# Four weight columns of a dense layer by seven products instead of eight, in four of six token groups

## The chip, the cores and the metric

The kernel runs on one core of one Trainium2 chip. The metric is the device time of one execution in microseconds. One execution was taken by the hardware profiler; its events are what the profile shows. The engines are named as in the profile: PE (TensorE, matrix multiplication), PEld (its weight loads, which overlap with PE), DVE (VectorE), ACT (ScalarE), POOL (GpSimd) and SP (SyncE, here only a queue of DMAs). Each engine takes its own instructions in the order in which the program lists them.

## The reference

A linear attention with decay (4 batches, 8 heads, 768 tokens, head size 64) and, on its output, a two-layer network with the Mish activation.

```
for each block of 64 tokens:
    intra = (q k^T * Dmask) v                  # Dmask = lam^(i-j) for i >= j
    inter = (q * lam^(pos+1)) kv_state
    out   = intra + inter
    kv_state = lam^64 * kv_state + (k * lam^(63-pos))^T v
x = out, heads joined                           # 3072 tokens x 512
h = x @ w_in                                    # 512 x 2048, the first dense layer
g = h * tanh(softplus(h))                       # Mish
result = g @ w_out                              # 2048 x 512, the second dense layer
```

## The kernel before

The tokens are cut into six groups (n = 0 to 5) of 128 positions x 4 batches = 512 tokens. The kernel's attention works on blocks of 128 positions, so a group is four chunks (i = 4n + b), one for each batch. `xt[n]` holds the attention's output of group n, turned so that the 512 model columns lie on partitions (4 chunks of 128, `kc`). `hsg[n]` holds the first layer's output after Mish: 16 units of 128 columns, times 512 tokens.

**Order.** The program is written out by hand (`tc.manual_schedule()`): the order in which the Python code calls things is the order on each engine. The main loop over groups goes through a list `units`, and after unit u it does the other work that is due there.

**A group, n of 1 to 5, before.** Units 0 to 7 are *duos* (`mm1_duo`): two of the 16 column units (2g and 2g+1) for the first half of the tokens, 8 matmuls of 256 columns into one PSUM bank, then one Mish on ACT. Units 8 to 15 are the same for the second half of the tokens. Units 16 to 29 are the second layer (`fast_unit`): it is done already by seven products P1 to P7 instead of eight (Strassen's scheme in Winograd's form, over halves of the tokens, the inner dimension and the columns), in the order P1, P5, P6, P2, P7, P3, P4, each as two blocks of 8 matmuls. It needs sums of weights (`tsum`, `weight_sum`, once) and of activations (`gsum`, `token_sum`, each group), which DVE makes. Partial results are copied by ACT from one PSUM bank to another, on which the next product then accumulates, for example `z<-x` after P1 and `y<-z` after P6.

**Attention for the next group** lies between the units (`visit`, `turns`). `turn(i)` scales one chunk of k on DVE (`scale_k`) and issues two transposing DMAs on SP (`qraw`, `kraw`). `pair_s` does the scores of two chunks: 16 matmuls into four PSUM banks, 16 more into `pO` from the state, and four masks (`sb`) on DVE. `pair_o` adds the values: 16 matmuls, four DVE operations (`xtok`) and two transposing DMAs into `xt`. `pair_a` brings the state forward: 8 matmuls into two banks (`pv`), four DVE sums of them with the old state (`raw`) and one more (`state`).

**PSUM** is eight banks, given out by tags: "ph" (2), "po" (2), "pS", "pk", "pO", "pq" (1 each). A tag's next tile waits until the one before is read. In units below 15, `pair_s` and `pair_a` use the two "po" banks (`spare`); `pair_s` uses "pS" and "pk" for its first chunk.

**Group 0** has whole units of 512 tokens (`mm1_unit`) and is preceded by the first attention chunks (`look_t`, `look_s`, `look_o`, `look_kv`), in which PE often waits for ACT and DVE; short matmuls on zeros (`busy`) fill such waits. The weight sums `tsum` are made by DVE around units 14 to 23 of group 0. Inputs and weights are loaded by POOL's DMA queue; `pace()` lets POOL wait for a marker in `hsg` before later loads.

Of the kernel before, what the change touches and what calls it, by code (L numbers as in the profile page):

```python
# [7 lines left out]
F32 = mybir.dt.float32  # L8
# [12 lines left out]
def kernel(  # L21
# [12 lines left out]
    C = 128  # L34
# [166 lines left out]
    kq = {}  # L201
    sbs = {}

    def look_t(i, between=0, mid=None):

        out_ = []
        for src, name in ((k0 if i == 0 else kn[i] if i < B else ktil[i], "pk"),
                          (q0 if i == 0 else qn[i], "pq")):
            pt = ps.tile([128, JP, C], F16, name=name, tag=name)
            for j in range(JP):  # L210
                nc.tensor.matmul(
                    pt[:, j, :], src[:, 2 * j : 2 * j + 2, :].rearrange("p h c -> p (h c)"), ident,
                    is_transpose=True, start=(j == 0), stop=(j == JP - 1),
                )
            out_.append(work.tile([128, JP, C], F16, name=f"{name}T", tag=f"{name}T", bufs=2))
            if name == "pk" and between:
                busy(between, C)
            if name == "pq" and mid:
                mid()
            if name == "pq" and i >= B:  # L220
                nc.vector.tensor_tensor(out=out_[-1], in0=pt, in1=lq, op=ALU.mult)
            elif name == "pq" and i in (0, 3):
                nc.vector.tensor_copy(out_[-1], pt)
            else:
                nc.scalar.activation(out_[-1], pt, AF.Copy)
        kq[i] = out_

    def look_s(i, hold=False):

        kT, qT = kq[i]  # L230
        pS = [ps.tile([128, JP, C], F32, name="pS", tag=g, bufs=m)
              for g, m in (("pS", 1), ("po", 2) if i < B else ("pk", 1))]
        for j in range(JP):
            for t in range(2):
                rs = slice(64 * t, 64 * t + 64)
                nc.tensor.matmul(pS[t][:, j, :], kT[rs, j, :], qT[rs, j, :],  # L236
                                 start=(j == 0), stop=(j == JP - 1), skip_group_check=True)
        sbs[i] = [None, None]

        def mask(t):  # L240
            sbs[i][t] = work.tile([128, JP, C], F16, name="sb", tag="sb", bufs=4)
            nc.vector.tensor_tensor(out=sbs[i][t], in0=pS[t],
                                    in1=dm[:, t] if i < B else bc(maskT, 1, JP), op=ALU.mult)

        masks = [lambda t=t: mask(t) for t in ((0, 1) if i < B else (1, 0))]
        if hold:
            return masks
        for f in masks:
            f()

    def look_o(i):

# [208 lines left out]
    def weight_sum(i, s):  # L461
# [7 lines left out]
        )[i]  # L469
        nc.vector.tensor_tensor(out=tsum[i][:, ks, :], in0=a, in1=b, op=op)  # L470

    gsum = {}

    def token_sum(n, i, part):

        if (n, i) not in gsum:
            gsum[n, i] = work.tile([128, HK, 2 * C], F16, name=f"gsum{i}", tag=f"gsum{i}", bufs=1)
        w = HK // 2
        ks = slice(part * w, part * w + w)
        kh = slice(HK + part * w, HK + part * w + w)  # L480
        h = hsg[n]
        lo, hi = slice(0, 2 * C), slice(2 * C, 4 * C)
        a, b, op = (
            lambda: (h[:, ks, hi], h[:, kh, hi], ALU.add),
            lambda: (gsum[n, 0][:, ks, :], h[:, ks, lo], ALU.subtract),
            lambda: (h[:, ks, lo], h[:, ks, hi], ALU.subtract),
            lambda: (h[:, kh, lo], gsum[n, 1][:, ks, :], ALU.subtract),
        )[i]()
        nc.vector.tensor_tensor(out=gsum[n, i][:, ks, :], in0=a, in1=b, op=op)  # L489
# [118 lines left out]
    busy(3)  # L608
    look_s(1)
    q_powers()  # L610
    for hp in range(2):
        rs = slice(64 * hp, 64 * hp + 64)
        nc.vector.tensor_copy(lbm[rs, :, rs], bc(lbc[rs, :], 2, D))
    look_o(0)
    look_t(2)
    q_decays()
    busy(2)
    masks = look_s(2, hold=True)
    look_o(1)
    look_t(3, mid=masks[0])  # L620
    masks[1]()
    nc.scalar.preload_act_table(AF.Mish)
    busy(1)
    look_s(3)
# [3 lines left out]
    look_o(3)  # L628
    for i in range(1, B):
        scale_k(i)  # L630
    summed()
    busy(2)

# [8 lines left out]
    for u, (fn, args) in enumerate(units):  # L642
        put_off = []
        fn(*args, **({"then": put_off} if u in (23, 25) else {}))
        if u < B - 1:
            look_kv(u + 1, "pq" if u == 0 else "po")()
        if 8 <= u < 8 + NVB - B:
            nc.vector.memset(vz[u - 8 + B][:, :, D : 2 * D], 0.0)
        elif u == 13:
            nc.vector.tensor_scalar(out=maskT, in0=rel, scalar1=0.0, scalar2=None, op0=ALU.is_ge)  # L650
        for i, s in {14: ((0, 0),), 15: ((0, 1),), 18: ((1, 0), (2, 0)),
                     20: ((1, 1), (2, 1))}.get(u, ()):
            weight_sum(i, s)
        for i, part in sums.get(u, ()):
            token_sum(0, i, part)
        if u == 22:
            scale_k(4)
            weight_sum(3, 0)
        then = [f(i, "po" if i == 5 else "ph") if f is look_kv else f(i) for f, i in visit.get(u, ())]
        if u == 23:  # L660
            scale_k(5)
            scale_k(6)
            weight_sum(3, 1)
        for f in put_off + then:
            if f:
                f()
        if u in (25, 26, 27):
            for _ in range(2):
                ahead.pop(0)()
        if u == 26:  # L670
            scale_k(7)
    next_state(1, 0)

    for n in range(1, NG):
        r, s, t = Pair(), Pair(), Pair()
        r.n, r.bs, s.n, s.bs, t.n, t.bs = n, (2, 3), n + 1, (0, 1), n + 1, (2, 3)
        visit = {}
        if n > 1:
            visit[0] = pair_o, last
        if 1 < n < NG - 1:  # L680
            visit[5] = pair_a, r
        if n < NG - 1:
            visit[9 if n > 1 else 11] = pair_s, s
            visit[16] = pair_o, s
            visit[26] = pair_s, t
        if n < NG - 2:
            visit[21] = pair_a, s
        last = t
        turns = {23: (n + 2) * B, 25: (n + 2) * B + 1}
        turns.update({1: 9, 4: 10, 7: 11} if n == 1 else {3: (n + 1) * B + 2, 6: (n + 1) * B + 3})  # L690
        units = [(mm1_duo, (n, g, lo, lo + GT // 2)) for lo in (0, GT // 2) for g in range(NKI // 2)]
        steps = ("P1", "P5", "P6", "P2", "P7", "P3", "P4")
        units += [(fast_unit, (n, step, blk)) for step in steps for blk in range(2)]
# [5 lines left out]
        sums = {9: ((2, 0),), 11: ((2, 1),), NKI - 3: ((0, 0), (1, 0)), NKI - 1: ((0, 1), (1, 1)),  # L699
                NKI + 4: ((3, 0),), NKI + 5: ((3, 1),)}  # L700
        for u, (fn, args) in enumerate(units):
            fn(*args)
# [11 lines left out]
            if later and (8 <= u < 16 or u in (17, 19, 21, 23)):  # L714
                pace()
                later.pop(0)()
            for i, part in sums.get(u, ()):
                token_sum(n, i, part)
            if turns.get(u, NG * B) < NG * B:
                turn(turns[u])  # L720
            if u in visit:
                f, s_ = visit[u]
                s_.spare = ("po", "po") if u < NKI - 1 else ("pS", "pk") if f is pair_a else ("ph", "po")
                f(s_)


# [28 lines left out]
```

## Time and profile before

| | |
|---|---|
| median of 3 runs (lowest, highest) | 201.9 us (201.06, 202.19) |
| profiled execution | 201.82 us |
| its span, from the first to the last instruction | 200.0 us |
| outside the span | 1.82 us |
| granted PE clock over the span | 1.00 |
| busy: PE, PEld, DVE, ACT, POOL | 192.7, 161.0, 132.7, 91.7, 81.7 us |

On the chain of waits, group 1 begins at 50.5 us, group 2 at 81.0, group 3 at 110.8, group 4 at 140.7 and group 5 at 170.0; the last matmul ends at 196.8. A row of the groups of instructions reads: line, engine, operation, out<-in with shapes, count | busy us, mean ns of one | idle time of the engine just before them, and what ended it. A row of the timeline or of the chain begins with its start and its length in us. "x4" in a timeline row means four instructions merged, whose length runs from the first start to the last end.

### The profile page before, as it was taken

Reading aid. Unit: us, or ns where it says so; the run is one execution under the profiler, and the core shown is the slowest. Engines: PE = TensorE matmul, PEld = TensorE weight load, DVE = VectorE, ACT = ScalarE, POOL = GpSimd, SP = SyncE. Lnnn points to the kernel's source line nnn. Section 1 sums busy time; section 2 is a strip of 40 time slices with the busy share of each in tenths; the row PEclk is TensorE's granted clock in tenths of the full one; section 3 lists DMA queues with packets and bytes.
Section 4 is the critical chain, followed back from the end, with each engine's and each line's share of the span. In section 5 each row is a group of like instructions: output and inputs, shape, how many; then the busy total and the mean of one; then the engine's idle time right before and its main releaser. Section 6 shows DMA issues by size and latency. Waiting matters only on the chain.

```text
span 200.0 us, 5052 instructions
## 1 busy us (share of the span) xinstructions
PE 192.7 (96%) x2081; PEld 161.0 (80%) x2081; DVE 132.7 (66%) x251; ACT 91.7 (46%) x158; POOL 81.7 (41%) x129
## 2 busy tenths in 40 slices
PE   7969999999999999999999999999999999999993
PEld 3645447878888998998998998998998988988882
DVE  7798359799935978657878557878557827305513
ACT  5694674323665421465420565430565430666230
POOL 7996333778488862007982007982000000000000
PEclk9999999999999999999999999999999999999999
DMA  9999999999999999999999959999991023500014
GB/s 131 143 143 194 206 207 202 154 173 198 194 102 151 158 149 165 176 241 71 109 140 198 231 106 79 99 103 178 267 120 35 0 56 105 156 6 0 3 52 157
DMA packets 112457, 26.81 MB, mean 134 GB/s; under 512 B 101554, under 2 KB 112434, under 8 KB 112434
## 3 DMA queue, kind: packets, MB, share of 16 engines
q0 software_dynamic: 77552, 13.37, 98.7%
q1 hardware_dynamic: 30848, 9.97, 29.4%
q10 hardware_dynamic: 4034, 3.15, 5.5%
q8 instruction: 16, 0.26, 0.6%
q14 instruction: 7, 0.06, 0.1%
HBM read 27.26 MB, written 6.29 MB: 168 GB/s over the span
## 4 chain that ended last, share of the span: by engine, by line
PE 93%; DVE 3%; ACT 2%; issue 0%; ACTq 0%
PE ph L443 35%; PE z L503 14%; PE x L503 10%; PE ph L414 7%; PE y L503 6%; PE w L503 5%; PE pS L358 2%; PE pO L264 2%; PE pO L385 2%; PE pS L236 1%; PE pv L337 1%; DVE dm L177 1%; PE busy L157 1%; PE pO L366 1%; PE pv L311 1%; PE fin L578 1%
## 5 line engine op out<-in xcount | busy, mean ns | idle before, releaser
L443 PE MATMUL ph<-xt,win 128*128 128x256 f16 x640 | 72.9, 273 | 0.0
L443 PEld LDWEIGHTS <-win 128*128 128x128 f16 x640 | 61.6, 98 | 7.4
L450 ACT ACTIVATE hsg<-ph 128x512 f16<-128x512 f32 x80 | 47.8, 597 | 29.3 <-PE ph L443 29.2
L503 PEld LDWEIGHTS <-gsum 128*128 128x128 f16 x384 | 36.9, 98 | 4.8 <-DVE tsum L470 0.3
L489 DVE TENSOR_TENSOR gsum<-hsg 128x1024 f16<-128x1024 f16 x24 | 16.6, 691 | 23.8 <-ACT hsg L450 18.5
L503 PEld LDWEIGHTS <-hsg 128*128 128x128 f16 x272 | 26.1, 98 | 3.2
L503 PE MATMUL x<-wout,hsg 128*128 128x256 f16 x192 | 23.7, 273 | 0.0
L67 POOL DMA_DIRECT2D kn<-in_k_dram x23 | 20.6, 894 | 7.4 <-DMA win<-in_moe_w_in_dram 2.2
L503 PE MATMUL z<-tsum,gsum 128*128 128x256 f16 x192 | 23.3, 273 | 0.0
L405 POOL COPY paced<-hsg 1x1 f16<-1x1 f16 x33 | 10.4, 314 | 31.5 <-ACT hsg L450 31.5
L75 POOL DMA_DIRECT2D qn<-in_q_dram x23 | 20.4, 888 | 6.0 <-DMA wout<-in_moe_w_out_dram 3.3
L78 POOL DMA_DIRECT2D vz<-in_v_dram x24 | 21.2, 886 | 3.4 <-DMA wout<-in_moe_w_out_dram 1.7
L374 DVE TENSOR_TENSOR sb<-pS,maskT 128x512 f16<-128x512 f32 x32 | 19.9, 684 | 1.0 <-PE pS L358 0.7
L297 DVE TENSOR_TENSOR raw<-pv,state 64x256 f32<-64x256 f32 x24 | 10.1, 422 | 12.8 <-PE pv L337 12.5
L274 DVE TENSOR_TENSOR ktil<-kn,lk 128x512 f16<-128x512 f16 (+1 forms) x22 | 14.9, 684 | 3.0 <-DMA kn<-in_k_dram 3.0
L414 PE MATMUL ph<-xt,win 128*128 128x512 f16 x64 | 14.5, 379 | 0.3 <-ACT xt L266 0.3
L393 DVE TENSOR_TENSOR xtok<-pO,lqt 128x256 f16<-128x256 f32 x32 | 11.3, 416 | 3.9 <-PE pO L385 3.9
L560 ACT ACTIVATE osum<-z 128x512 f32<-128x512 f32 x5 | 3.0, 597 | 23.6 <-PE z L503 23.6
L530 DVE TENSOR_TENSOR osum<-z,p 128x512 f32<-128x512 f32 x6 | 4.1, 690 | 12.9 <-issue 6.8
L503 PE MATMUL y<-wout,gsum 128*128 128x256 f16 x96 | 12.3, 273 | 0.0
L426 ACT ACTIVATE hsg<-ph 128x512 f16<-128x512 f32 x16 | 9.6, 597 | 5.8 <-PE ph L414 5.8
L414 PEld LDWEIGHTS <-win 128*128 128x128 f16 x64 | 6.1, 98 | 7.3 <-issue 0.4
(93 smaller groups left out, 209.0 us busy)
## 6 DMA issues: line engine op xcount, KB each, us to landing
vz<-in_v_dram POOLq DMA_DIRECT2D x24, 128.0 KB, 6.8
out_dram<-osum SPq DMA_DIRECT2D x12, 256.0 KB, 5.2
kn<-in_k_dram POOLq DMA_DIRECT2D x23, 128.0 KB, 5.8
qn<-in_q_dram POOLq DMA_DIRECT2D x23, 128.0 KB, 5.8
out_dram<-osum ACTq DMA_DIRECT2D x11, 256.0 KB, 4.6
wout<-in_moe_w_out_dram POOLq DMA_DIRECT2D x4, 512.0 KB, 16.7
win<-in_moe_w_in_dram POOLq DMA_DIRECT2D x3, 512.0 KB, 10.3
win<-in_moe_w_in_dram POOLq DMA_DIRECT2D x2, 256.0 KB, 6.4
```

Of the source, the lines that this page charges most:

```text
L67: nc.gpsimd.dma_start(out=kn[i], in_=chunk_rows(k, i))
L75: nc.gpsimd.dma_start(out=qn[i], in_=chunk_rows(q, i))
L78: nc.gpsimd.dma_start(out=vz[i % NVB][:, :, 0:D], in_=chunk_rows(v, i))
L274: (nc.gpsimd if B + 1 < i < 2 * B else nc.vector).tensor_tensor(out=t, in0=kn[i], in1=bc(lk, 2, D), op=ALU.mult)
L374: nc.vector.tensor_tensor(out=s.sb[m][t], in0=sc[m][t], in1=bc(maskT, 1, JP), op=ALU.mult)
L393: nc.vector.tensor_tensor(out=xtok[m][:, :, t, :], in0=s.pO[t][:, m], in1=bc(lt[:, :, t], 2, D), op=ALU.mult)
L405: nc.gpsimd.tensor_copy(paced, mark[-1])
L414: nc.tensor.matmul(ph_t[ni][:, lo:hi], w_in(ni, kc), xt[n][:, kc, lo:hi], start=(kc == 0), stop=(kc == NKC - 1),)
L443: nc.tensor.matmul(t[:, m, lo - half * h : hi - half * h], w_in(ni, kc), xt[n][:, kc, lo:hi], start=(m == 0 and kc == 0), stop=(kc == NKC ...
L450: nc.scalar.activation(hsg[n][:, 2 * g : 2 * g + 2, half * h : half * h + h], t, AF.Mish)
L489: nc.vector.tensor_tensor(out=gsum[n, i][:, ks, :], in0=a, in1=b, op=op)
L503: nc.tensor.matmul(places(n, key)[:, blk, lo:hi], lhs(kk, blk), rhs(kk, lo, hi), start=(fresh and kk == 0 and blk == 0), stop=(kk == HK - ...
```

## The change

In groups 2 to 5, column units 12 to 15 (the weight tile `win1536`, 512 x 512) are no longer four duos of the list. They are one 512 x 512 x 512 multiplication by seven products, `set_unit`, in the same scheme as the second layer: halves of the tokens, of the inner dimension and of the columns. A product is 4 matmuls of 256 columns. Group 1 keeps its duos.

- `in_sum` makes four weight sums (128 x 512 elements, f16) on DVE once, in group 0 after unit 12, ahead of `tsum`.
- `x_sum` makes four sums of `xt` (128 x 512, f16) on DVE in each of the groups, two after unit 6 and two after unit 8, behind that unit's visit.
- The group has 28 list entries: 0 to 3 duos of the first half; 4 is P1 and a duo, 5 is P2 and a duo; 6 to 9 duos of the second half; 10 is P5 and P6, 11 a duo, 12 is P7 and P3, 13 a duo and P4; 14 to 27 the second layer.
- Copies on ACT: after P1 the bank x to SBUF (`u1`); after P5 the bank w to SBUF (`p5`); ahead of P6 `u1` into bank z; after P6 bank z into bank y. Then P7 and P4 accumulate on z, P3 on y. DVE adds `p5` to z after P7 and to y after P3 (`hs`), and Mish reads those sums; after P2 and P4 it reads the bank itself.
- Visits move to fit: `pair_s` for the next group's first pair comes after unit 6 (it was 9), with `pair_a` after unit 5 as before. The closing `pair_o` of the second pair comes after the last unit of a group, and no longer after unit 0 of the next. The second `turn` comes after unit 5 (it was 6), and the token sums of the halves come together after unit 13.
- In the opening, the two `lbm` copies on DVE move from before `look_o(0)` to behind the first `scale_k`, and both masks of chunk 2 stand together ahead of the pq copy of chunk 3 (one stood behind it). `weight_sum(3, 1)` moves from unit 23 to unit 25 of group 0.

The diff, cut to its core:

```diff
-    def look_t(i, between=0, mid=None):
+    def look_t(i, between=0):
...
-            if name == "pq" and mid:
-                mid()
...
+    KH = NKC // 2
+    SU = NKI - 4
+    isum = [const.tile([128, KH, 256], F16, name=f"isum{i}") for i in range(4)]
+    def i_quarter(r, c):
+        t = win[-1]
+        return t[:, r * KH : (r + 1) * KH, c * 256 : (c + 1) * 256]
+    def in_sum(i):
+        a, b, op = (
+            lambda: (i_quarter(0, 1), i_quarter(0, 0), ALU.subtract),
+            lambda: (i_quarter(1, 1), isum[0], ALU.subtract),
+            lambda: (i_quarter(1, 1), i_quarter(0, 1), ALU.subtract),
+            lambda: (i_quarter(1, 0), isum[1], ALU.subtract),
+        )[i]()
+        nc.vector.tensor_tensor(out=isum[i], in0=a, in1=b, op=op)
+    def x_sum(n, i):
+        xsum[n, i] = work.tile([128, KH, 2 * C], F16, name=f"xsum{i}", tag=f"xsum{i}", bufs=1)
+        x = xt[n]
...
+        a, b, op = (
+            lambda: (x[:, k0_, hi], x[:, k1_, hi], ALU.add),
+            lambda: (xsum[n, 0], x[:, k0_, lo], ALU.subtract),
+            lambda: (x[:, k0_, lo], x[:, k0_, hi], ALU.subtract),
+            lambda: (x[:, k1_, lo], xsum[n, 1], ALU.subtract),
+        )[i]()
+        nc.vector.tensor_tensor(out=xsum[n, i], in0=a, in1=b, op=op)
+    def set_unit(n, step):
...
+        key, lhs, rhs = {
+            "P1": lambda: ("x", w_quarter_(0, 0), x_quarter(0, 0)),
+            "P2": lambda: ("x", w_quarter_(1, 0), x_quarter(0, 1)),
+            "P6": lambda: ("z", w_part_(1), x_part(1)),
+            "P5": lambda: ("w", w_part_(0), x_part(0)),
+            "P7": lambda: ("z", w_part_(2), x_part(2)),
+            "P3": lambda: ("y", w_quarter_(1, 1), x_part(3)),
+            "P4": lambda: ("z", w_part_(3), x_quarter(1, 1)),
+        }[step]()
+        def place(key):
+            if (n, key) not in first:
+                tag, bufs = {"x": ("po", 2), "z": ("po", 2), "w": ("pS", 1), "y": ("pk", 1)}[key]
+                first[n, key] = ps.tile([128, 2, 2 * C], F32, name=f"s{key}", tag=tag, bufs=bufs)
+            return first[n, key]
...
+        if step == "P6":
+            nc.scalar.activation(place("z"), first[n, "u1"], AF.Copy)
+        t = place(key)
+        for m in range(2):
+            for kk in range(KH):
+                nc.tensor.matmul(
+                    t[:, m, :], lhs(kk, m), rhs(kk),
+                    start=(step in ("P1", "P5") and m == 0 and kk == 0), stop=(kk == KH - 1),
+                    skip_group_check=True)
+        if step == "P1":
+            kept("u1", t, "osb", 4)
+        elif step == "P2":
+            mish(n, 0, 0, t)
+        elif step == "P5":
+            kept("p5", t, "p5", 1)
+        elif step == "P6":
+            nc.scalar.activation(place("y"), t, AF.Copy)
+        elif step == "P7":
+            plus_(1, "z")()
+        elif step == "P3":
+            plus_(0, "y")()
+        elif step == "P4":
+            mish(n, 1, 0, t)
...
+        d = 0 if n == 1 else 2
         if 1 < n < NG - 1:
             visit[5] = pair_a, r
         if n < NG - 1:
-            visit[9 if n > 1 else 11] = pair_s, s
-            visit[16] = pair_o, s
-            visit[26] = pair_s, t
+            visit[6 if d else 11] = pair_s, s
+            visit[16 - d] = pair_o, s
+            visit[26 - d] = pair_s, t
+            visit[29 - d] = pair_o, t
...
+        if d:
+            units = [[duo(g, 0)] for g in range(4)]
+            units += [[part("P1"), duo(4, 0)], [part("P2"), duo(5, 0)]]
+            units += [[duo(g, 1)] for g in range(4)]
+            units += [[part("P5"), part("P6")], [duo(4, 1)], [part("P7"), part("P3")], [duo(5, 1), part("P4")]]
...
+            sums = {13: ((0, 0), (0, 1), (1, 0), (1, 1)), 17: ((2, 0),), 18: ((2, 1),), 20: ((3, 0),), 21: ((3, 1),)}
...
+            if d and u in (6, 8):
+                for i in (0, 1) if u == 6 else (2, 3):
+                    x_sum(n, i)
```

More of the change, by code (lines that the diff above doesn't have):

```diff
@@ L226, in look_t, with look_s @@
         kq[i] = out_
-    def look_s(i, hold=False):
+    def look_s(i):
         kT, qT = kq[i]
@@ L238, in look_s @@
         sbs[i] = [None, None]
-        def mask(t):
+        for t in (0, 1) if i < B else (1, 0):
             sbs[i][t] = work.tile([128, JP, C], F16, name="sb", tag="sb", bufs=4)
@@ new lines, with mish, x_quarter, x_part @@
+    first = {}
+    def mish(n, r, c, src):
+        nc.scalar.activation(
+            hsg[n][:, SU + 2 * c : SU + 2 * c + 2, r * 2 * C : (r + 1) * 2 * C], src, AF.Mish)
+        mark.append(hsg[n][0:1, SU + 2 * c, r * 2 * C : r * 2 * C + 1])
+    def set_unit(n, step):
+        def x_quarter(r, c):
+            return lambda kk: xt[n][:, c * KH + kk, r * 2 * C : (r + 1) * 2 * C]
+        def x_part(i):
+            return lambda kk: xsum[n, i][:, kk, :]
+        def w_quarter_(r, c):
+            return lambda kk, m: i_quarter(r, c)[:, kk, m * 128 : (m + 1) * 128]
+        def w_part_(i):
+            return lambda kk, m: isum[i][:, kk, m * 128 : (m + 1) * 128]
+        key, lhs, rhs = {
[12 more added lines that the diff above has]
+            return first[n, key]
+        def kept(key, src, tag, bufs):
+            first[n, key] = work.tile([128, 2, 2 * C], F32, name=key, tag=tag, bufs=bufs)
+            nc.scalar.activation(first[n, key], src, AF.Copy)
+        def plus_(r, key):
+            o = work.tile([128, 2, 2 * C], F32, name="hs", tag="hs", bufs=2)
+            nc.vector.tensor_tensor(out=o, in0=first[n, key], in1=first[n, "p5"], op=ALU.add)
+            return lambda: mish(n, r, 1, o)
+        if step == "P6":
[21 more added lines that the diff above has]
+            mish(n, 1, 0, t)
@@ L610 @@
     q_powers()
-    for hp in range(2):
-        rs = slice(64 * hp, 64 * hp + 64)
-        nc.vector.tensor_copy(lbm[rs, :, rs], bc(lbc[rs, :], 2, D))
     look_o(0)
@@ L617 @@
     busy(2)
-    masks = look_s(2, hold=True)
+    look_s(2)
     look_o(1)
-    look_t(3, mid=masks[0])
-    masks[1]()
+    look_t(3)
     nc.scalar.preload_act_table(AF.Mish)
@@ L630 @@
         scale_k(i)
+    for hp in range(2):
+        rs = slice(64 * hp, 64 * hp + 64)
+        nc.vector.tensor_copy(lbm[rs, :, rs], bc(lbc[rs, :], 2, D))
     summed()
@@ L655 @@
             token_sum(0, i, part)
+        if u == NKI - 4:
+            for i in range(4):
+                in_sum(i)
         if u == 22:
@@ L662 @@
             scale_k(6)
+        if u == 25:
             weight_sum(3, 1)
@@ L682, with duo, part @@
         if n < NG - 1:
-            visit[9 if n > 1 else 11] = pair_s, s
-            visit[16] = pair_o, s
-            visit[26] = pair_s, t
+            visit[6 if d else 11] = pair_s, s
+            visit[16 - d] = pair_o, s
+            visit[26 - d] = pair_s, t
+            visit[29 - d] = pair_o, t
         if n < NG - 2:
[L687 to L691, printed above, removed]
+            visit[21 - d] = pair_a, s
+        turns = {23 - d: (n + 2) * B, 25 - d: (n + 2) * B + 1}
+        turns.update({3: (n + 1) * B + 2, 5: (n + 1) * B + 3} if d else {1: 9, 4: 10, 7: 11})
+        def duo(g, half):
+            return mm1_duo, (n, g, half * (GT // 2), (half + 1) * (GT // 2))
+        def part(step):
+            return set_unit, (n, step)
+        if d:
[3 more added lines that the diff above has]
+            units += [[part("P5"), part("P6")], [duo(4, 1)], [part("P7"), part("P3")], [duo(5, 1), part("P4")]]
+        else:
+            units = [[duo(g, half)] for half in range(2) for g in range(NKI // 2)]
         steps = ("P1", "P5", "P6", "P2", "P7", "P3", "P4")
-        units += [(fast_unit, (n, step, blk)) for step in steps for blk in range(2)]
+        units += [[(fast_unit, (n, step, blk))] for step in steps for blk in range(2)]
         later = []
@@ L698 @@
                 (load_v, 0), (load_v, 1), (load_k, 3), (load_q, 3), (load_v, 2), (load_v, 3))]
[L699 to L702, printed above, removed]
+        if d:
+            slots = *range(6, 14), 15, 17, 19, 21
+            sums = {13: ((0, 0), (0, 1), (1, 0), (1, 1)), 17: ((2, 0),), 18: ((2, 1),), 20: ((3, 0),), 21: ((3, 1),)}
+        else:
+            slots = *range(8, 16), 17, 19, 21, 23
+            sums = {9: ((2, 0),), 11: ((2, 1),), NKI - 3: ((0, 0), (1, 0)), NKI - 1: ((0, 1), (1, 1)),
+                    NKI + 4: ((3, 0),), NKI + 5: ((3, 1),)}
+        for u, calls in enumerate(units):
+            for fn, args in calls:
+                fn(*args)
             if n == 1 and u == 0:
@@ L713 @@
                 ahead.pop(0)()
-            if later and (8 <= u < 16 or u in (17, 19, 21, 23)):
+            if later and u in slots:
                 pace()
```

12 lines of the change are left out of this document (4 added, 8 removed).

## The prediction

> **What bounds the kernel now.** I read the page's busy times and chain first, then the stretches of single groups, the groups of instructions, and last the order in time at the places that the edit touches. The page:
>
> ```profile
> PE 192.7 (96%) x2081; PEld 161.0 (80%) x2081; DVE 132.7 (66%) x251; ACT 91.7 (46%) x158; POOL 81.7 (41%) x129
> PE 93%; DVE 3%; ACT 2%; issue 0%; ACTq 0%
> ```
>
> TensorE (PE) is busy for 96% of the span and carries 93% of the chain that ended last. The stretches show one steady group and five microseconds of the opening:
>
> ```profile
> 10.00:15.00 5.00, 3.29 (x50) 2.31 (x47) 4.90 (x11) 4.70 (x8) 5.00 (x8) 1.00 1.87 143
> 110.84:140.66 29.82, 29.82 (x355) 26.62 (x353) 21.43 (x41) 12.51 (x21) 14.05 (x24) 1.00 1.52 129
> ```
>
> Columns: stretch, its length, then PE, PEld, DVE, ACT and POOL busy, then granted clock. In the steady group PE has no gap at all (29.82 of 29.82), at full clock; DVE has 8 us free and ACT 17. So two things decide: fewer matmuls shorten the span one for one, and any new wait of PE lengthens it one for one. In a gapless stream nothing absorbs a wait. Only the opening has waits already.
>
> **The part that gains.** Units 12 to 15 of one group take 32 matmuls of 256 columns now (four duos of 8) and 28 after (seven products of 4). What one costs in the stream, and what stands around it:
>
> ```profile
> 86.74 0.45 PE pv L337 x8
> 87.19 3.49 PE ph L443 x32
> 90.68 0.55 PE pS L358 x16
> 91.23 0.23 PE pO L366 x16
> ```
> ```profile
> L443 PE MATMUL ph<-xt,win 128*128 128x256 f16 x640 | 72.9, 273 | 0.0
> L393 DVE TENSOR_TENSOR xtok<-pO,lqt 128x256 f16<-128x256 f32 x32 | 11.3, 416 | 3.9 <-PE pO L385 3.9
> L489 DVE TENSOR_TENSOR gsum<-hsg 128x1024 f16<-128x1024 f16 x24 | 16.6, 691 | 23.8 <-ACT hsg L450 18.5 <-ACT hsg L426 5.2
> L503 PEld LDWEIGHTS <-gsum 128*128 128x128 f16 x384 | 36.9, 98 | 4.8 <-DVE tsum L470 0.3
> L549 ACT ACTIVATE p<-w 128x512 f32<-128x512 f32 x6 | 3.6, 597 | 7.2 <-PE w L503 7.2
> L539 ACT ACTIVATE z<-x 128x512 f32<-128x512 f32 x6 | 3.5, 582 | 8.8 <-PE x L503 8.8
> ```
>
> 3.49/32 = 0.109 us per matmul, a duo of 8 is 0.873, a product of 4 is 0.437. Four groups lose 4 matmuls each: 16 x 0.109 = **-1.75**. One matmul lasts 0.273, so its result comes 0.273 - 0.109 = 0.164 after the next could start; a wait on a result costs that too.
>
> **P6 behind two copies (the largest term).** Units run P5 and P6 back to back, with nothing between. P6 adds onto U1 in the z bank, and ScalarE (ACT) puts U1 there by a copy that is issued behind the copy of P5's product to SBUF. So P6, next on PE, waits for P5's end, then copy, then copy; queued behind it on PE are the duo, P7, P3 and all else. In the second layer the same steps stand 16 matmuls apart, which hides them. The trace holds the same shape in the opening: a PE end, one or two ACT copies, PE again.
>
> ```profile
> 10.43 0.59 ACT pkT L225
> 11.02 0.50 ACT pqT L225
> ...
> 11.56 0.40 PE pS L236 x8
> ...
> 12.98 0.69 DVE sb L242
> 13.68 0.34 DVE pqT L223
> ...
> 14.06 0.40 PE pS L236 x8
> ...
> 15.89 0.62 PE pO L264 x8
> ...
> 16.54 0.61 ACT xt L266
> ...
> 17.19 1.02 PE ph L414 x4
> ```
>
> ACT starts 16.54 - 16.51 = 0.03 to 0.04 after PE's end; two copies end 0.59 + 0.50 = 1.09 after the first began, and PE starts 0.04 later (1.13). With L539's 0.58 as the second it is about 1.12. So the stall is 0.164 + 0.04 + 1.12 = **1.33** in groups 2 to 4, and 0.06 more in group 5, where the ACT of the duo before is still running at P5's end (its 0.597 begins 0.20 after P5 does, and P5 is through at 0.60): 1.39. Sum 3 x 1.33 + 1.39 = **+5.38**. Bounds: one copy alone exposed, 0.164 + 0.04 + 0.58 + 0.05 = 0.83, and 1.6 if ACT starts late. The Trainium skill ("ScalarE: Activation LUTs", "What ACT_TABLE_LOAD costs") gives 186 ns + 0.833 ns per element and an overlap of about 93 ns for neighbours: two copies of 512 would be 1.13, not the trace's 1.09, and the sum 0.2 higher; the row decides.
>
> **P2 behind U1.** P2 adds onto the bank that ACT first copies out as u1, behind the ACT of the duo before. That ACT starts 0.20 after P1 begins, u1 0.50 later, done 1.30 after P1 began; P1 and the duo between last 1.31. With the 0.04 to PE: 0.06 late, 4 times: **+0.24** (bounds 0 and 0.6).
>
> **Pair_s one unit behind pair_a (groups 2 to 4).** Both take the two "po" banks. Before, three to four units lay between; now one duo. What reads pair_a's banks:
>
> ```profile
> 87.00 1.75 DVE L297 TENSOR_TENSOR raw<-pv,state 64x256 f32<-64x256 f32 x4 [2.81 <-PE pv L337]
> 88.78 0.69 DVE L302 TENSOR_TENSOR state<-raw,lbc 128x512 f16<-128x512 f32 x1
> ...
> 92.07 2.48 DVE L374 TENSOR_TENSOR sb<-pS,maskT 128x512 f16<-128x512 f32 x4
> ```
>
> Counted from pair_a's start (86.74): the four raw sums run from 0.26 to 2.01 and cannot start sooner. Pair_s, after 0.45 of pair_a, 0.87 of duo and 0.28 of its own first half, wants the banks at 1.60 and gets them at 2.05: 0.44 each, 3 times: **+1.32**. Bounds: 0, if DVE read the banks sooner, and 1.1, if the state sum had to end too. `turn` at unit 5 (unit 6 before) now stands ahead of these sums on DVE; its scale_k waits for nothing that PE does and runs before them, and its two transposes on SP follow earlier: free.
>
> **P5 behind x_sum (groups 2 to 4).** DVE takes its queue in order: raw, state, four masks, then x_sum 0. State starts at 2.04; the masks follow at 2.65 (four in 2.48, so 0.60 from start to start) and end at 5.13. An f16 sum of 1024 elements takes 0.69, the state sum of 512 f32 elements takes 0.69 too; so an f16 sum of 512 should be near L393's 0.42 for 256 f32 elements. x_sum 0 then ends at 5.47, and PE could start P5 at 5.53. PE itself is there after pair_s (2.52) and three duos (2.62), at 5.14. Stall 0.37, 3 times: **+1.11** (bounds 0, and 0.65 at 0.69 for the sum). x_sum 1 is done before P6's copies are, and x_sums 2 and 3 run under that stall: free. Group 5 has no pair_a or pair_s; its sums are free.
>
> **P7, P3, P4 and the end of the first layer.** The copy to y hides under the duo behind P6 (0.64 against 0.87), the sums for P7 and P3 (0.69 each) under P3 and the duo. ACT then has four Mish in a row at 0.50 each and ends 1.4 after P4; DVE follows with the token sums. P5 of the second layer stands 1.75 behind P4 and needs the second half at 2.18; it comes at 2.31. In groups 2 to 4 pair_o (0.47) lies between and covers it, in group 5 it shows: **+0.13** (bounds 0 and 0.7).
>
> **Group 0: in_sum.** Four new sums enter DVE at unit 12.
>
> ```profile
> 31.24 1.29 DVE L470 TENSOR_TENSOR tsum<-wout 128x1024 f16<-128x1024 f16 x2
> ...
> 34.56 0.68 DVE L470 TENSOR_TENSOR tsum<-wout,tsum 128x1024 f16<-128x1024 f16 x1
> ...
> 41.26 1.28 DVE L242 TENSOR_TENSOR sb<-pS,maskT 128x512 f16<-128x512 f32 x2
> ...
> 44.74 1.29 DVE L242 TENSOR_TENSOR sb<-pS,maskT 128x512 f16<-128x512 f32 x2
> ```
> ```profile
> 35.30 1.05 PE L503 MATMUL z<-tsum,gsum 128*128 128x256 f16 x8
> ...
> 42.00 0.38 PE L211 MATMUL pk<-ident,ktil 128*128 128x128 f16 x4 [0.40 <-DVE sb L242]
> ...
> 45.52 0.39 PE L211 MATMUL pk<-ident,ktil 128*128 128x128 f16 x4
> ```
>
> Between the first two rows lie three more sums of 0.69, which fill the time. The row at 34.56 ends at 35.24, and PE's P6 starts at 35.30: no slack, as PEld's wait for tsum (0.3) says. Four sums of 0.42, 0.33 apart and one of them behind its own input, push it by 3 x 0.33 + 0.46 = **+1.45** (bounds 0.8, if part is absorbed, and 2.3, at 0.60 each). The moved weight_sum(3, 1) (0.60 of DVE) frees the wait at 42.00, and then stands ahead of the masks at 44.74, whose first (0.69) releases the pk at 45.52 with 0.05 to spare: what is won is given back. 0 (bounds -0.57 and +0.2).
>
> **The opening.** The lbm copies leave DVE ahead of the masks of chunk 2.
>
> ```profile
> 11.56 1.39 DVE L613 COPY lbm<-lbc 64x256 f32<-64x256 f32 x2
> ```
> ```profile
> 16.71 0.10 PEld L414 LDWEIGHTS <-win 128*128 128x128 f16 x1 [0.27 <-DMA win<-in_moe_w_in_dram]
> ```
>
> Both masks can start at 12.00 (PE's pS ends at 11.96) and end at 13.29; the pqT copy ends at 13.6 and look_s(3) starts at 13.67, not 14.06. Its masks end near 15.4, so look_o(3) and the xt copy come 0.45 sooner. But the first unit's weights, which arrive by DMA, load until 16.81, so it starts at 16.84, not 17.19: **-0.35** (bounds 0 and -0.48). The copies, in their new place, end near 18.5 on a DVE with room. Pair_o one unit sooner saves nothing: PE does the same work in another order.
>
> **Sum.** -1.75 + 5.38 + 0.24 + 1.32 + 1.11 + 0.13 + 1.45 - 0.35 = +7.53. The profiled execution took 201.82 (span 200.0 and 1.82 around it), 0.1 under the median of 201.9; so 209.35, I say **209.3 us**.
>
> **The rivals.**
>
> *All waits hidden.* If ACT put U1 into its bank while P5 still runs, and DVE were ahead, only -1.75 - 0.35 is left: 199.7. It decides where the copy to z stands ahead of P5's own on ACT. In its order it stands behind. 4%.
>
> *Only P6 waits.* DVE's sums are all covered: -1.75 - 0.35 + 5.38 + 0.24 = +3.5, 205.3. For it speaks that DVE is idle for 8 us of a group; against it, that the queue is full just there. 14%.
>
> *More waits.* The second half of xt is needed six units after pair_o:
>
> ```profile
> L395 SPq DMA_TRANSPOSE xt<-xtok x2: 1191/1206/1220, 172.0 to 173.2; - x2
> DMA to landing us min/median/max: 2.6/3.3/4.0
> ```
> ```profile
> 170.90 0.47 PE pO L385 x16
> 171.36 13.13 PE ph L443 x120
> ```
>
> In group 5 it lands at 173.2 + 4.0 = 177.2; it is wanted seven duos after pair_o, at 171.36 + 6.11 = 177.47. The margin is 0.3, and pair_o now runs 0.87 nearer behind the stores. With 0.6 lost there in two groups, sums at 0.69 (0.9 in group 0, 0.8 for x_sum) the time is 211.9. 17%.
>
> *The clock falls.* The new gaps of a group stand close together. If they halved the granted clock for 32 matmuls (3.49), that would cost 3.5 in each of four groups, 14 in all: 223. Against it, PE was busy for only 3.29 of 5.00 us in the opening at a granted 1.00, and no new gap is longer than 1.4. 2%. The Trainium skill ("TensorE: Matmul & The Clock Gate", "Part 1: The HAM clock gate") has the clock halve after an idle window of about 3.4 us; by that rule too it would stay up.
>
> My forecast has the other 63%.
>
> **How the numbers follow.** The range goes from the second rival (205.3) to the third (211.9): **205.3 to 211.9**; outside lie the first, the last and half of each of those two, some 2 in 10. This kernel's measurement can tell 0.5%, 1.0 us. Only the first rival is faster: 0.05 with a little for what I do not see; within 0.5%, some mixture of it with one hidden copy: 0.03; slower: 0.92.
>
> **What would show it.** Right: P6 (sz) waits for ACT some 1.3 us in each of groups 2 to 5, pair_s for DVE raw and sw for xsum 0.4 in three of them, w and z of group 0 for DVE; groups 2 to 4 last 1.7 longer than before, group 5 1.1. Wrong: no ACT wait ahead of sz, or a group shorter than before; then the order of ACT's copies does not bind as I read it.

## The result and the profile after

The changed kernel takes 209.91 us (median of 6 runs, 209.29 to 210.05), beside 202.05 for the kernel before (median of 6 runs, 201.06 to 202.42): ratio 1.0388, interval 1.0369 to 1.0407. It is slower by 7.9 us, and inside the range. The profiled execution took 209.93, its span 208.2. Two runs of the kernels below that lay far above the others of their kernel (205.96 and 691.81 us) are left out of the ratios.

The page's busy times and its chain:

```profile
PE 193.2 (93%) x2065; PEld 158.9 (76%) x2065; DVE 142.6 (69%) x279; ACT 98.9 (48%) x174; POOL 81.1 (39%) x129
...
PE 21%; ACT 1%; issue 0%; DVE 0%
```

There are 16 matmuls fewer, and still PE's busy time is 0.5 us up, since a row counts a matmul from its start to its modelled end and overlapping ones once: behind each new gap a row starts afresh. The span grew by 8.2, so PE's share falls to 93%. The chain is of little use here: its shares add up to 22%, because it was followed back only as far as 159.7 us. The places where PE stood are in the waits (who waited for whom: us in total, how often, the longest):

```profile
PE sz L550 <- ACT sz L546: 4.8, 4, 1.2
...
PE pS L349 <- DVE raw L288: 1.1, 3, 0.4
...
PE sw L550 <- DVE xsum L496: 0.7, 3, 0.2
PE w L600 <- DVE gsum L586: 0.6, 1, 0.6
PE z L600 <- DVE tsum L461: 0.6, 1, 0.6
PE pk L211 <- DVE sb L239: 0.4, 1, 0.4
```

A wait like the last, of 0.40, stood in the trace before too, at the pk one step sooner; that one is gone now. The others are new. L550 is set_unit's matmul, L546 its copy of U1 into the z bank, L349 pair_s, L496 the sum over x, L600 the second layer; w and z are both of group 0. The columns count from the end of the matmul before; the time lost against a gapless stream is 0.164 more where a result had to drain. Two groups by the stretches (length, then PE, PEld, DVE, ACT, POOL busy, then granted clock), the first from unit 0 of group 2 to unit 0 of group 3, the second from unit 0 of group 5 to the end of its PE work:

```profile
82.67:114.37 31.70, 29.95 (x355) 26.19 (x352) 23.45 (x46) 14.37 (x26) 13.85 (x24) 1.00 1.27 138
177.32:204.88 27.56, 26.32 (x250) 22.96 (x246) 11.20 (x22) 14.60 (x26) 0.00 (x0) 1.00 0.17 50
```

The steady group was 29.82 long with PE busy throughout; it is 31.70 now with PE busy for 29.95, at a granted 1.00. PE in order of time in group 2 shows where it stands:

```profile
86.60 1.04 PE L434 MATMUL ph<-xt,win 128*128 128x256 f16 x8
87.50 0.60 PE L550 MATMUL sx<-xt,win 128*128 128x256 f16 x4
...
90.22 0.45 PE L349 MATMUL pS<-qraw,kraw 64*128 64x128 f16 x9
91.03 0.40 PE L349 MATMUL pS<-qraw,kraw 64*128 64x128 f16 x7 [0.36 <-DVE raw L288]
...
91.59 2.79 PE L434 MATMUL ph<-xt,win 128*128 128x256 f16 x24
94.60 0.60 PE L550 MATMUL sw<-xsum,isum 128*128 128x256 f16 x4 [0.22 <-DVE xsum L496]
96.38 0.60 PE L550 MATMUL sz<-xsum,isum 128*128 128x256 f16 x4 [1.18 <-ACT sz L546]
96.81 1.04 PE L434 MATMUL ph<-xt,win 128*128 128x256 f16 x8
```

P5 (94.60) should be through at 95.04; P6 starts at 96.38, 1.34 later. Between lie the two copies of ACT, one behind the other:

```profile
95.23 0.60 ACT L538 ACTIVATE p<-sw 128x512 f32<-128x512 f32 x1 [0.21 <-PE sw L550]
95.73 0.60 ACT L546 ACTIVATE sz<-u 128x512 f32<-128x512 f32 x1
```

P5 itself comes 0.39 after the three duos are through (91.59 + 2.62 = 94.21). Pair_s takes 1.37 from 90.22 to 91.59, where it took 0.79 before (90.61 to 91.40 in the timeline): 0.58 lost. P2 (87.50) stands 0.03 behind the duo. Together with the four matmuls saved (-0.44) that is +1.90 for a group; the periods between the unit 0 of groups 2, 3, 4 and 5 grew by 1.89, 1.88 and 1.89. The P6 waits of groups 2 to 4 are alike; that of group 5 is 1.38 (186.96 + 0.44 to 188.78).

In group 0 DVE takes the four new sums (the first and the last are shown), and PE waits there and at a pk; DVE, then PE:

```profile
31.18 0.42 DVE L480 TENSOR_TENSOR isum<-win 128x512 f16<-128x512 f16 x1
...
32.31 0.42 DVE L480 TENSOR_TENSOR isum<-win,isum 128x512 f16<-128x512 f16 x1
...
36.04 0.69 DVE L461 TENSOR_TENSOR tsum<-wout,tsum 128x1024 f16<-128x1024 f16 x1
```
```profile
36.78 1.05 PE L600 MATMUL z<-tsum,gsum 128*128 128x256 f16 x8 [0.57 <-DVE tsum L461]
...
46.99 0.38 PE L211 MATMUL pk<-ident,ktil 128*128 128x128 f16 x4 [0.39 <-DVE sb L239]
```

P6 of the second layer starts at 36.78 instead of 35.30.

### The profile page after: what moved, and what is told of

It reads as the page before. It is cut to its first block, busy times and chain, and to the rows that moved or that the text cites. A ratio compares the mean times of both kernels' runs of the same rounds, so it can differ in the third digit from the quotient of the medians.

```text
span 208.2 us, 5077 instructions
## 1 busy us (share of the span) xinstructions
PE 193.2 (93%) x2065; PEld 158.9 (76%) x2065; DVE 142.6 (69%) x279; ACT 98.9 (48%) x174; POOL 81.1 (39%) x129
## 5 line engine op out<-in xcount | busy, mean ns | idle before, releaser
L434 PE MATMUL ph<-xt,win 128*128 128x256 f16 x512 | 60.9, 273 | 0.0
L434 PEld LDWEIGHTS <-win 128*128 128x128 f16 x512 | 49.1, 98 | 5.9
L441 ACT ACTIVATE hsg<-ph 128x512 f16<-128x512 f32 x64 | 38.1, 596 | 24.9 <-PE ph L434 24.8
L600 PEld LDWEIGHTS <-gsum 128*128 128x128 f16 x384 | 36.5, 98 | 6.8 <-DVE gsum L586 1.1
L600 PEld LDWEIGHTS <-hsg 128*128 128x128 f16 x272 | 26.0, 98 | 3.3
L586 DVE TENSOR_TENSOR gsum<-hsg 128x1024 f16<-128x1024 f16 x24 | 15.8, 687 | 12.9 <-ACT hsg L441 7.6
L600 PE MATMUL z<-tsum,gsum 128*128 128x256 f16 x192 | 23.3, 273 | 0.6 <-DVE tsum L461 0.6
L600 PE MATMUL x<-wout,hsg 128*128 128x256 f16 x192 | 23.7, 273 | 0.0
L396 POOL COPY paced<-hsg 1x1 f16<-1x1 f16 x33 | 8.9, 270 | 34.8 <-ACT hsg L441 33.8
L542 DVE TENSOR_TENSOR hs<-sz,p 128x512 f32<-128x512 f32 x4 | 2.8, 692 | 15.5 <-PE sz L550 15.5
L600 PE MATMUL w<-tsum,gsum 128*128 128x256 f16 x96 | 11.8, 273 | 0.6 <-DVE gsum L586 0.6
L600 PE MATMUL y<-wout,gsum 128*128 128x256 f16 x96 | 12.3, 273 | 0.0
L417 ACT ACTIVATE hsg<-ph 128x512 f16<-128x512 f32 x16 | 9.6, 597 | 5.8 <-PE ph L405 5.8
L550 PEld LDWEIGHTS <-isum 128*128 128x128 f16 x64 | 6.2, 96 | 7.4 <-issue 6.2
```

The lines of the kernel that those rows point to most:

```text
L417: nc.scalar.activation(hsg[n][:, ni, :], ph_t.pop(ni), AF.Mish)
L434: nc.tensor.matmul(t[:, m, lo - half * h : hi - half * h], w_in(ni, kc), xt[n][:, kc, lo:hi], start=(m == 0 and kc == 0), stop=(kc == NKC ...
L441: nc.scalar.activation(hsg[n][:, 2 * g : 2 * g + 2, half * h : half * h + h], t, AF.Mish)
L600: nc.tensor.matmul(places(n, key)[:, blk, lo:hi], lhs(kk, blk), rhs(kk, lo, hi), start=(fresh and kk == 0 and blk == 0), stop=(kk == HK - ...
```

## The experiments

The first four kernels are the changed one with one edit each, run beside one another and beside the kernel before (202.19 in that company); the ratios are to that.

**The copy of U1 into the z bank taken out of P5's way** (e1_z_copy_early). A step Z of its own, after unit 8, does the copy; nothing of it is left under P6.

```diff
-        if step == "P6":
+        if step == "Z":
             nc.scalar.activation(place("z"), first[n, "u1"], AF.Copy)
+            return
...
+            if d and u == 8:
+                set_unit(n, "Z")
```

> The changed kernel with one ACT copy moved: U1 goes into bank z after unit 8, not between P5 and P6. Theory A (the copies ahead of P6 are the largest loss, and nothing else is late behind them): the four waits of sz for ACT (4.8 us in the profile, 5.4 with PE's drain) go, and the time falls from 209.9 to about 204.5. Rival B (the wait only covers the next one: P6 then waits for x_sum 1, P7 for the copy to y, or the token sums at the end of the layer come late): less than half comes back, 207 or more.

204.87 us, ratio 1.0129 (1.0107 to 1.0151): 5.0 less than the changed kernel. PE's waits no longer have sz; pair_s and sw wait as before:

```profile
PE pS L349 <- DVE raw L288: 1.1, 3, 0.4
...
PE ph L405 <- DMA win<-in_moe_w_in_dram: 0.7, 1, 0.7
PE sw L552 <- DVE xsum L496: 0.7, 3, 0.2
```

So the stall ahead of P6 is most of the loss, and it comes from the place of one copy in ACT's queue, not from the seven products.

**The same copy just ahead of P5** (e4_z_copy_before_p5). The step Z as above, but inside the unit.

```diff
-            units += [[part("P5"), part("P6")], [duo(4, 1)], ...
+            units += [[part("Z"), part("P5"), part("P6")], [duo(4, 1)], ...
```

> The same copy moved by one step only: it is issued just ahead of P5's matmuls, so that on ACT it stands behind the Mish of unit 9 and ahead of P5's own copy. Theory A counts by ACT's queue: P6 is free when the Mish and one copy are over, a stall of 0.5 instead of 1.34 in groups 2 to 4 and of 0.9 instead of 1.4 in group 5: 3 x 0.82 + 0.5 = 3.0 less, 206.9. Rival B: no difference to the run with the copy after unit 8, or none to the changed kernel.

206.66 us, ratio 1.0231 (1.0196 to 1.0267): 3.25 less. ACT still has the copy behind the Mish of the duo before P5, and P6 waits for that copy alone:

```profile
PE sz L552 <- ACT sz L547: 1.8, 4, 0.7
```

The 4.8 us of waits become 1.8: it is the number of ACT's steps between P5's end and P6 that sets the stall.

**Pair_a three units sooner** (e2_pair_a_early).

```diff
-            visit[5] = pair_a, r
+            visit[2] = pair_a, r
```

> The changed kernel with pair_a of groups 2 to 4 after unit 2, not after unit 5. Theory A (the raw sums on DVE make both pair_s and, through the masks and x_sum 0, P5 late): both waits go, 3 x (0.58 + 0.39) = 2.9 less, 207.0. Rival B (the masks and x_sum are late by themselves): only pair_s gains, 1.7 less, 208.2. Rival C (PE's wait ahead of P6 grows by what P5 gains): no more than 1.7 less as well, but with sw not waiting and sz waiting longer.

207.35 us, ratio 1.0256 (1.0238 to 1.0274): 2.6 less. Pair_s and P5 now start without a named wait, and the group from P6 to P6 takes 126.41 - 95.53 = 30.88 instead of 31.70:

```profile
91.02 2.79 PE L434 MATMUL ph<-xt,win 128*128 128x256 f16 x24
93.76 0.60 PE L550 MATMUL sw<-xsum,isum 128*128 128x256 f16 x4
95.53 0.60 PE L550 MATMUL sz<-xsum,isum 128*128 128x256 f16 x4 [1.18 <-ACT sz L546]
```

Both waits were one queue's: with the raw and state sums done three units sooner, the masks and the x sums move up too. What is left is a gap too short to be listed, 0.12 ahead of P5 (91.02 + 2.62 = 93.64).

**The sums over w_in moved to group 1** (e3_in_sum_late).

```diff
-        if u == NKI - 4:
-            for i in range(4):
-                in_sum(i)
...
+            if n == 1 and u in (18, 19):
+                for i in (0, 1) if u == 18 else (2, 3):
+                    in_sum(i)
```

> The changed kernel with the four in_sums in group 1 (after units 18 and 19), not in group 0. Theory A: DVE has no slack in group 0, and PE gets back the 1.40 that group 0 is longer: 208.5. Rival B: the moved weight_sum or the scale_k make DVE just as late behind it, and less than 0.7 comes back.

208.99 us, ratio 1.0337 (1.0318 to 1.0355): only 0.92 less. The waits of w and z are gone, as every theory wanted, but another one grew from 0.39 to 0.93:

```profile
45.94 0.38 PE L211 MATMUL pk<-ident,ktil 128*128 128x128 f16 x4 [0.93 <-DVE sb L239]
```

DVE and POOL at that place:

```profile
41.97 0.69 DVE L219 TENSOR_TENSOR pqT<-pq,lq 128x512 f16<-128x512 f16 x1
42.58 1.22 DVE L461 TENSOR_TENSOR tsum<-wout,tsum 128x1024 f16<-128x1024 f16 x1
...
45.20 1.29 DVE L239 TENSOR_TENSOR sb<-pS,maskT 128x512 f16<-128x512 f32 x2
```
```profile
42.21 1.04 POOL L265 TENSOR_TENSOR ktil<-kn,lk 128x512 f16<-128x512 f16 x1 [1.47 <-PE pv L302]
```

The moved weight_sum(3, 1) takes 1.22 instead of 0.68 where it now meets POOL's product, and it stands ahead of the masks that release pk. Without those 0.54 us the saving would have been some 1.46; that is an estimate from the two waits, 0.93 and 0.39.

The next four were run beside the kernel before (202.16 in that company). The first two put one part of the change alone into the kernel before.

**Pair_s alone** (e6_pair_s_alone): no product, no new sum.

```diff
-            visit[9 if n > 1 else 11] = pair_s, s
+            visit[6 if n > 1 else 11] = pair_s, s
...
-            turns.update({1: 9, 4: 10, 7: 11} if n == 1 else {3: (n + 1) * B + 2, 6: (n + 1) * B + 3})
+            turns.update({1: 9, 4: 10, 7: 11} if n == 1 else {3: (n + 1) * B + 2, 5: (n + 1) * B + 3})
```

> The kernel before with one visit moved: pair_s of groups 2 to 4 after unit 6 (it was 9), with its second turn after unit 5; no seven products. Theory A (pair_s is late because DVE's raw sums hold the two po banks, whatever the units are): pS waits for DVE raw in three groups as in the changed kernel, 0.58 each, 1.7 in all, 203.9. Rival B (the po bank of the seven products, or their ACT copies, make it late): no wait, 202.1.

204.03 us, ratio 1.0099 (1.0062 to 1.0137): +1.87, three times 0.6 (0.4 to 0.9 by the interval), in a kernel with none of the rest. The wait stands as it did in the changed kernel:

```profile
PE pS L358 <- DVE raw L297: 1.1, 3, 0.4
```

**The opening alone** (e5_opening_alone): the lbm copies behind the scale_k loop, the masks of chunk 2 no longer split around look_t(3).

```diff
-    for hp in range(2):
-        rs = slice(64 * hp, 64 * hp + 64)
-        nc.vector.tensor_copy(lbm[rs, :, rs], bc(lbc[rs, :], 2, D))
...
-    masks = look_s(2, hold=True)
+    look_s(2)
-    look_t(3, mid=masks[0])
-    masks[1]()
+    look_t(3)
...
+    for hp in range(2):
+        rs = slice(64 * hp, 64 * hp + 64)
+        nc.vector.tensor_copy(lbm[rs, :, rs], bc(lbc[rs, :], 2, D))
```

> The kernel before with the opening of the changed one (lbm copies later, both masks of chunk 2 together) and nothing else. The prediction's step says 0.35 less, 201.7; the comparison of the two traces says nothing gained, because ACT (the exp of lq ahead of pkT, the table load ahead of the xt copy) and the arrival of the first weights end last there: 202.1.

202.16 us, ratio 0.9993 (0.9977 to 1.0009): no difference that can be told. The interval reaches from 0.46 us less to 0.18 more, so the 0.35 of the prediction's step is not ruled out. Its trace does start unit 0 sooner, and loses it again in the second layer, where DVE and then PE stand for the last weights to land:

```profile
16.56 1.02 PE L414 MATMUL ph<-xt,win 128*128 128x512 f16 x4 [0.25 <-ACT xt L266]
...
37.41 1.03 PE L503 MATMUL z<-tsum,gsum 128*128 128x256 f16 x8 [0.81 <-DVE tsum L470]
```
```profile
36.66 0.69 DVE L470 TENSOR_TENSOR tsum<-wout,tsum 128x1024 f16<-128x1024 f16 x1 [1.44 <-DMA wout<-in_moe_w_out_dram]
```

**All three repairs together** (e7_all): the changed kernel with the early copy, pair_a at unit 2 and the sums over w_in in group 1.

> The changed kernel with three moves together: U1 into bank z after unit 8, pair_a after unit 2, in_sum in group 1. Theory A (the waits lie at different places and add): 209.9 - 5.0 - 2.6 - 0.9 = 201.4, and of the waits only the one of pk for the masks in group 0 and the one of w in group 5 are left. Rival B (with P5 on time, P6 meets x_sum 1 and P7 the copy to y): one or two waits of 0.1 to 0.5 in each group more, 202.5.

202.02 us, ratio 0.9982 (0.9959 to 1.0005). The forecast of 201.4 was missed by 0.6. None of the new waits of groups 2 to 5 is listed any more, but the rival is right in a small way: each of groups 2 to 4 lasts 29.63, where 29.37 would be left, and P5, P6 and P7 still start late by 0.12, 0.03 and 0.06 (the next run shows such gaps). What else is left is in group 0: the pk wait, as in the run with the sums in group 1 (0.92 here, 0.93 there), and, in the profiled execution, 0.60 of z behind the last w_out. The runs lay between 200.9 and 202.7, a little wider than those of the others; the landing of w_out could make that, which no run shows.

**And weight_sum(3, 1) behind the masks of unit 26** (e8_all_ws).

```diff
-        if u == 25:
-            weight_sum(3, 1)
...
+            weight_sum(3, 1)
```

> The same three moves and weight_sum(3, 1) after the masks of unit 26 in group 0, so that it stands behind the masks that release the pk bank. Theory A: the wait of pk (0.9 in the run with in_sum in group 1, 1.1 with the restart) goes, 200.3, faster than the kernel before by the 1.75 of the 16 matmuls that are left out. Rival: the pq copy or the P4 of group 0 comes late in its place, 201.0 or more.

201.11 us, ratio 0.994 (0.9919 to 0.9961) to the kernel before: this beats both kernels, by 1.05 and by 8.8 us of their medians. The 200.3 of theory A was not reached. The wait of pk is gone, but the rival is right in part, since the pq copy now comes late behind the moved sum. That is the one wait of PE that is left behind the opening (0.17, and 0.33 counted from start to start):

```profile
PE pS L234 <- DVE pqT L219: 0.2, 1, 0.2
```

The steady group:

```profile
81.08:110.71 29.63, 29.63 (x354) 26.04 (x351) 23.47 (x46) 14.11 (x26) 13.28 (x24) 1.00 1.39 147
```

PE is gapless by this view, yet the group is only 0.19 shorter than 29.82, not 0.44. PE in order of time has the rest in gaps that are shorter than a matmul's drain and so count as busy:

```profile
89.45 2.79 PE L434 MATMUL ph<-xt,win 128*128 128x256 f16 x24
92.19 0.60 PE L552 MATMUL sw<-xsum,isum 128*128 128x256 f16 x4
...
93.10 1.04 PE L434 MATMUL ph<-xt,win 128*128 128x256 f16 x8
94.03 0.60 PE L552 MATMUL sz<-xsum,isum 128*128 128x256 f16 x4
```

P5 starts 0.12 after the duos (89.45 + 2.62 = 92.07), P7 0.06 after its duo (93.10 + 0.87 = 93.97). In group 5 the four matmuls less save only 0.06: P7 starts 0.18 late there, and a product of the second layer behind the token sums 0.17.

The last two edit e8_all_ws and were run beside the kernel before (202.40 in that company).

**Each P5 computed twice** (e10_p5_twice): 16 matmuls more, the count of the kernel before.

```diff
-        for m in range(2):
-            for kk in range(KH):
+        for m, kk in [(m, kk) for _ in range(2 if step == "P5" else 1) for m in range(2) for kk in range(KH)]:
```

> The version with all moves (U1's copy, pair_a, in_sum and weight_sum moved) in which each P5 of the first layer is computed twice into the same bank, so that the units take 32 matmuls again, as the duos did; the result is the same. Theory A: with the waits gone PE is full, and a matmul costs its 0.109 us: 16 x 0.109 = 1.75 more than the version with all moves, 202.9. Rival: the small waits that are left behind P5 (its copies on ACT, the copy to y) had eaten part of what the products save, and the added matmuls fill them: less than 1.2 more.

202.60 us, ratio 1.0017 (1.0000 to 1.0033), against 0.994 without: 0.0077 of 202 is 1.55 us (1.0 to 2.1 by the two intervals). The steady group:

```profile
81.33:111.32 29.99, 29.99 (x358) 26.51 (x355) 23.46 (x46) 14.22 (x26) 13.31 (x24) 1.00 1.34 153
```

It is 0.36 longer, of 0.44 that four matmuls take; the four groups together are 1.35 longer in the traces. So the sum lies nearer to theory A's 1.75 than to nothing, though the intervals do not rule out the rival's 1.2. Once hardly anything waits, a product left out is worth most of its matmuls.

**The x sums ahead of pair_s's masks** (e9_x_sum_first): x_sum 0 and 1 are issued before pair_s instead of behind it, to close the 0.12 ahead of P5.

> The version with all moves, and x_sum 0 and 1 ahead of pair_s's masks on DVE, not behind them. In the version with all moves x_sum 0 ends 0.05 before P5 starts, and a group is 29.63 long where 29.37 would be left after four matmuls less. Theory A: P5 starts 0.1 sooner in three groups, 200.8 against 201.1. Rival: no difference, or the sums now wait for the transposes of xt and make the masks and the closing units late, 201.1 or more.

201.07 us, ratio 0.9947 (0.9929 to 0.9965): no different from 0.994. The gap did close and opened again three rows on:

```profile
89.25 2.79 PE L434 MATMUL ph<-xt,win 128*128 128x256 f16 x24
91.88 0.60 PE L552 MATMUL sw<-xsum,isum 128*128 128x256 f16 x4
...
92.78 1.04 PE L434 MATMUL ph<-xt,win 128*128 128x256 f16 x8
93.83 0.60 PE L552 MATMUL sz<-xsum,isum 128*128 128x256 f16 x4
```

P5 follows at once (89.25 + 2.62 = 91.87), and P7 now stands 1.05 behind its duo's start instead of 0.93. What it waits for is ACT's copy to y, which ends at 93.78, 0.05 ahead of it (93.98 and 94.03 in the run before):

```profile
93.17 0.61 ACT L563 ACTIVATE sy<-sz 128x512 f32<-128x512 f32 x1
```

## Why the prediction was right

The time, the sign and the places of the waits came out as put. Two terms of the sum, pair_s and the opening, were mis-sized by 0.42 each; smaller ones took 0.19 back, and the rest is the difference from 209.3 to 209.9.

| term | forecast | in the trace after |
|---|---|---|
| 16 matmuls fewer | -1.75 | taken as -1.75; 1.55 by P5 twice (1.0 to 2.1) |
| P6 behind two copies | +5.38 | 3 x 1.34 + 1.38 = +5.40 |
| P2 behind u1 | +0.24 | 4 x 0.03 = +0.12 |
| pair_s behind raw | +1.32 | 3 x 0.58 = +1.74 |
| P5 behind x_sum 0 | +1.11 | 3 x 0.39 = +1.17 |
| token sums, group 5 | +0.13 | +0.17 |
| sums over w_in, group 0 | +1.45 | +1.40 |
| opening | -0.35 | +0.07 |
| group 1 | 0 | -0.14 |
| sum | +7.53 | +8.18, of 8.2 in the span |

*P6.* The step was right in kind and size, and two runs show it: away with the copy's place, 5.0 us go; with one ACT step less, 3.25. The row taken from the opening (two copies in 1.09) carried the largest term.

*Pair_s.* The wait, its cause and its three places were right; the size, 0.44, was not. The step took pair_a's start from the chain (86.74) and the raw sums from the timeline (87.00 to 88.75), and so had the banks free 2.01 after pair_a's start. But a row of the chain begins where the one before it has ended. In the timeline before pair_a starts at 86.58, so the sums end 2.17 after it:

```profile
86.58 0.61 PE L337 MATMUL pv<-vz,ktil 128*128 128x128 f16 x8
```

After, it is the same: the sums end at 90.97, 2.16 after pair_a, and PE goes on at 91.03, where without a wait it would have gone on at 90.46.

```profile
88.81 0.61 PE L328 MATMUL pv<-vz,ktil 128*128 128x128 f16 x8
89.23 1.74 DVE L288 TENSOR_TENSOR raw<-pv,state 64x256 f32<-64x256 f32 x4 [3.98 <-PE pv L328]
```

So pair_s loses 0.58 in each group, and 0.62 by pair_s alone (1.87 / 3).

*P5.* Its size was in part luck. Counted from pair_a's start, x_sum 0 ended at 5.73 and not at 5.47, and PE was there at 5.40 and not at 5.14. Both readings were 0.26 too early, and the difference came out.

*The opening.* The step let look_s(3) follow the masks of chunk 2 and named DVE as what held it. Two things were overlooked. In this trace ACT was later than DVE: its pkT copy ended at 14.02, and look_s(3) started at 14.07. Behind that copy ACT loads its table, and only then copies xt, which look_o(3) waits for:

```profile
13.43 0.59 ACT L223 ACTIVATE pkT<-pk 128x512 f16<-128x512 f16 x1
14.03 1.28 ACT L715 ACT_TABLE_LOAD   x1
15.32 0.60 ACT L257 ACTIVATE xt<-pO 128x512 f16<-128x512 f32 x1
```

And times of one execution, the landing of the weights (16.81) above all, were taken as if they were fixed. From the start of look_s(1) to the end of the last xt copy of the opening it takes 8.19 in the trace before, 8.05 after and 7.89 in the opening alone, so 0.30 of the forecast's gain do show in that last trace. But look_s(1) starts anywhere from 8.57 to 9.61 in the twelve traces, in the run with the early copy PE stood 0.7 us for w_in, and the opening alone lost its head start to w_out. What is left of the gain in the median, 0 or 0.35, no run here can tell.

*Group 0.* +1.40 as put. But that its removal would give it all back, as a term of a sum should, fell: 0.92 came back, since the moved weight sum ran into POOL. The forecast had the moved sum at nothing; with the in_sums gone its place costs 0.54, and e8_all_ws, which puts it behind the masks, gets that back and more (ratio 0.9982 to 0.994; the intervals just touch).

*Group 1.* The -0.14 is not the change's: group 1 took 30.49 in the trace before, but 30.35 with pair_s alone and with the opening alone, which leave it as it was.

*The rivals.* None came: no transpose was waited for, the new sums took 0.42 and not 0.69, and the clock stayed at 1.00 with PE standing for up to 1.23 at a time. The Trainium skill ("TensorE: Matmul & The Clock Gate", "Part 1: The HAM clock gate") puts the window for a halved clock at about 3.4 us of idling; the trace agrees as far as it goes, since no gap here comes near that. The parts that the third rival names (1.2, 0.9 and 0.8 on top of 209.3) add up to 212.2, not to its 211.9; the measured time is well below both.

## What to carry to other kernels

In a stream without gaps a smaller count of matmuls is worth at most its own length, here 1.75 us, and every hand-over to another engine costs from the end of the matmul to the start of the next: put a copy that the next product needs into the other engine's queue well ahead of the product before it. When an order is made tighter, go through each bank and ask who reads it last and what that engine has queued ahead; three small moves here (a copy, a pair, the sums over w_in) took back the 7.9 us of loss, and a fourth (one weight sum) made it a gain of about 1. A busy share of 100% does not mean that nothing is lost: gaps below a matmul's drain show only in the starts.

## What the hardware showed that was not expected

A sum of two f16 inputs on DVE took 1.22 us instead of 0.68 where POOL ran a product of two f16 tensors beside it (42.58 and 42.21 in the kernel with the late sums), and 1.21 in the kernel with all three repairs. A DVE product that reads one input from PSUM took its usual 0.68 wholly inside POOL's next product (47.00, in 46.76 to 47.85). In the changed kernel the two met the other way round: a DVE product of two f16 SBUF tensors (41.54) was running when POOL's began (41.93); it took its usual 0.68, and POOL's took 1.20 instead of 1.04. The Trainium skill ("VectorE: DVE Perf Modes", "Two Vector instructions with no wait between them") says that a vector instruction with two tensor inputs in SBUF reads the second through an interface that is shared with GpSimd. That section gives no price for the two together; the rows agree with it in kind. No run here tried the pair by itself, so the cause is argued and not shown.
